# The first loads of a one-core attention and GLU kernel: tile 0 in two column halves, tile 1 from the scalar queue, tiles 2 and 3 ahead of K's weight rows, nine dummy matmuls

## The chip, the core and the metric

The kernel runs on one core of a Trainium2 chip. The core has five engines that run their own instruction lists and meet at semaphores: TensorE (PE, the matrix array; PEld is its weight load), VectorE (DVE), ScalarE (ACT), GpSimd (POOL) and SyncE (SP, which here only issues DMAs). The metric is the device time of one execution in microseconds (us), given as the median of several runs. Times inside an execution are counted from the start of the profile's span.

## The reference

A layer norm without gain or bias feeds two branches, whose outputs are added to the input: attention over a sliding, dilated window (32 heads of 20, 8 positions 2 apart), and a bilinear gated unit without an activation.

```python
def _A_ref(x, wqkv, wo):                 # B, S, D = 1, 2048, 640
    qkv = (x @ wqkv).reshape(B, S, 3, H, Dh) ...
    q, k, v = qkv[0], qkv[1], qkv[2]
    off = jnp.arange(W) * dil            # W, dil = 8, 2
    idx = pos[:, None] - off[None, :]
    ...
    logits = einsum("bhsd,bhswd->bhsw", q, kg) * Dh ** -0.5
    attn = softmax(where(mask, logits, -1e9), axis=-1)
    o = einsum("bhsw,bhswd->bhsd", attn, vg)
    return o.reshape(B, S, D) @ wo

def _B_ref(x, w_gate, w_up, w_down):     # F = 1536
    return ((x @ w_gate) * (x @ w_up)) @ w_down

xn = _layernorm(x)
return x + _A_ref(xn, A_wqkv, A_wo) + _B_ref(xn, B_w_gate, B_w_up, B_w_down)
```

`A_x` is the input of both branches. All arrays are bfloat16.

## The kernel before

The 2048 rows are cut into 16 tiles of 128 rows (`t`), and four blocks of 512 rows (`j`). The 640 columns are five chunks of 128.

**A planner writes the order.** Nothing is issued by hand loops alone. `Sched` keeps, for each engine, a clock of its own (`K.t`), gives each operation an assumed occupancy (`occ`), and each DMA an assumed landing (`land`, where one is given). Threads yield tasks with priorities, and `run` always takes the task that can start first, with the priority deciding between those that are close. The outcome is a fixed list for each engine, with semaphore waits between them; on the chip every engine runs its list in order. So an assumed time costs no instruction, but a different one can change the order of all work behind it. DMAs issued directly, outside a task, stand at the point of the program where they are called.

**The stages.** `front(t)` normalizes a tile: two `bn_stats` of 320 columns each (L574) and an aggregate (L577) on DVE, a square root on ACT (L584), a reciprocal (L591) and the apply on DVE (L603 for tiles 0 and 1, in two pieces of 256 and 384 columns; L606 for tiles 2 to 5) or on ACT (L609, tiles 6 to 15). Tiles 0 to 3 are transposed on PE (L642) and copied from PSUM to `XNT` by ACT or DVE (L653, L655, L662); tiles 4 to 15 are transposed by a DMA on SP's queue (L675). The statistics of tile 1 are planned only after tile 0's apply.

`proj_qk` projects Q and K. For tiles 0 and 1 it uses `spread` (L730), 128 columns at a time, in two parts: chunks 0 and 1, then chunks 2 to 4, for each of the five output groups. Later tiles use L698, as V does. The rows of `wqkv` come in two loads for Q (`wqkv_load(0, ...)`) and two for K (`wqkv_load(1, ...)`): chunks 0 to 2 (480 KB) and chunks 3 and 4 (320 KB). A matmul waits for the load of its own chunk.

Then come the products of Q and K on DVE (L881, and L930 in single precision), their sums on POOL, and the logits on PE, where three blocks of L1013 matmuls reduce over the head dimension; the softmax; the weighted values (L1192 on DVE, added pairwise on POOL at L1197); four groups of L1251 matmuls on PE that sum over the window; the gate and up projections (L1315); and the down and output projections (L1416, L1467), accumulated in one PSUM bank. The gate, up and V projections and parts of the down projection serve as filler between the others.

**The head of the program.** Before the planner runs, the first DMAs are issued in a written order (L1521 to L1529): tile 0 on SP; a small read of `wqkv` (`touch`, 5 KB) on ACT's queue; then, all on SP, Q's first rows, tile 1, Q's last rows, K's first rows, tile 2, K's last rows. `loads` goes on with tile 3. `warm` (L682) puts ten matmuls of constants, 512 columns wide, on PE, into a PSUM bank that nobody reads; three narrower ones stand behind tile 0's transposes.

`x_load(t)` is one DMA of a tile's 128 rows of 640 columns, 160 KB, into a slot of `XST`.

Of the kernel before, what the change touches and what calls it, by code (L numbers as in the profile page):

```python
# [11 lines left out]
NCH = 5  # L12
# [9 lines left out]
TS = 128  # L22
JB = 512
HB = 1024
QB = 256
DHALF = D // 2
# [329 lines left out]
def build_kernel(nc, A_x, A_wqkv, A_wo, B_x, B_w_gate, B_w_up, B_w_down, out):  # L356
    K = Sched(nc)
# [4 lines left out]
    def sb(name, shape, dtype=BF16, at=None):  # L362
        n = mybir.dt.size(dtype)
        for s in shape[1:]:
            n *= s
        n = (n + 63) // 64 * 64
        if at is None:
            at = place[0]
            place[0] += n
        assert at + n <= 229344, (name, at + n)  # L370
        return K.sbuf(name, shape, dtype, at)
# [10 lines left out]
    NXS = 12  # L382
    XST = sb("XST", [128, NXS, D], at=a_ot + NCH * JB * 2)
# [77 lines left out]
    def mark(*k):  # L461
        done.add(k)
# [4 lines left out]
    def have(*k):  # L467
        return lambda: k in done

    def num(n, *k):  # L470
        return lambda: count.get(k, 0) >= n

    xhbm = A_x[0]
    ohbm = out[0]

    def dma(o, i, r=(), w=(), name="", eng="sp", group=None, land=None):
        n = mybir.dt.size(o.dtype)
        for s in o.shape:
            n *= s
        return op(eng, lambda e: e.dma_start(o, i), r=r, w=w, dma=True, name=name, nbytes=n, group=group, land=land)  # L480
# [6 lines left out]
       r=[IDENT[:]], w=[IDENT[:]], name="ident", occ=0.4)  # L487
    op("pool", lambda e: e.memset(SEL[:], 0.0), w=[SEL[:]], name="sel", occ=0.1)
    for q in range(4):
        op("pool", (lambda q: lambda e: e.affine_select(SEL[:], SEL[:], pattern=[[-1, 32]], compare_op=ALU.not_equal, fill=1.0,  # L490
                                                        base=-32 * q, channel_multiplier=1))(q),
           r=[SEL[:]], w=[SEL[:]], name=f"sel{q}", occ=0.2)
# [3 lines left out]
       r=[G[:]], w=[G[:]], name="g1", occ=0.3)  # L496
    op("pool", lambda e: e.affine_select(G[:], G[:], pattern=[[-4, H]], compare_op=ALU.is_ge,
                                         fill=0.0, base=0, channel_multiplier=1),
       r=[G[:]], w=[G[:]], name="g2", occ=0.3)
# [8 lines left out]
    def xslot(t):  # L508
        return t + 4 if t < 8 else t - 8

    def x_load(t, eng="sp", land=None):
        dma(XST[:, xslot(t), :], xhbm[t * TS:(t + 1) * TS, :], w=[XST[:, xslot(t), :]], name=f"xld{t}", eng=eng, land=land)
        mark("x", t)

    wqkv_src = A_wqkv.rearrange("(c p) n -> p c n", p=128)

    def wqkv_load(g, lo=0, hi=NCH, eng="sp", land=None):
        dst = WQKV[:, WPOS[g], lo:hi, :]
        dma(dst, wqkv_src[:, lo:hi, g * D:(g + 1) * D], w=[dst], name=f"ld_wqkv{g}_{lo}", eng=eng, land=land)

    def loads():
        def t(f, *a):
            return Task("sp", lambda: f(*a), prio=0)

        for t_ in range(3, NXS):
            yield t(x_load, t_)
        yield t(wqkv_load, 2)
        for t_ in range(NXS, NT):
            yield have("apply", t_ - NXS)
            yield t(x_load, t_)  # L530

        def w(T, src):
            dma(T[:], src.rearrange("(c p) n -> p c n", p=128), w=[T[:]], name="ld_w")

        def pads():
            z = ZERO[:, 0:PAD].unsqueeze(1).to_broadcast([128, NCH, PAD])
            dma(vscr[:, 0:PAD].rearrange("(c p) s -> p c s", p=128), z, r=[ZERO[:, 0:PAD]], w=[("vscr", "pad")], name="vpad")

        yield have("xnt", NT - 1)
        yield t(w, WG, B_w_gate)  # L540
        yield t(pads)
        yield t(w, WU, B_w_up)

        def copy_x():
            a, b = ohbm[0:3 * JB, :], xhbm[0:3 * JB, :]
            o, i = a.rearrange("(p r) n -> p (r n)", p=128), b.rearrange("(p r) n -> p (r n)", p=128)
            op("sp", lambda e: e.dma_start(o, i), w=[("outx",)], dma=True, name="outx", nbytes=2e6)

        yield num(2, "lg")
        yield t(copy_x)  # L550
# [15 lines left out]
    def front(t):  # L566
        x, st = XST[:, xslot(t), :], STATS[:, t, 0:12]
        xs, mv = XNS[:, t % NXN, :], MV[:, t, 0:2]
        sd, rstd, nmr = SD[:, t, 0:1], SD[:, t, 1:2], SD[:, t, 2:3]
        p = 0.1 * t  # L570

        def stats(i):
            o, a = st[:, 6 * i:6 * i + 6], x[:, i * DHALF:(i + 1) * DHALF]
            op("dve", lambda e: e.bn_stats(o, a), r=[a], w=[("st", t, i)], name=f"bn{t}_{i}", occ=0.49)  # L574
# [4 lines left out]
        ts = next((g for g in GROUPS if t in g), (t,))  # L579
        t0, t1 = ts[0], ts[-1] + 1  # L580

        def sqrt():
            o, i = SD[:, t0:t1, 0:1], MV[:, t0:t1, 1:2]
            op("act", lambda e: e.activation(o, i, ACT.Sqrt, bias=EPSC[:, 0:1]), r=[("mv", k) for k in ts] + [EPSC[:]],  # L584
               w=[("sd", k) for k in ts], name=f"sd{t}", occ=0.25)
            for k in ts:
                mark("sd", k)

# [27 lines left out]
        for i in range(2):  # L616
            if t == 2 and i == 0:
                yield have("apply", 1)
            if t == 2 and i == 1:
                yield have("xnt", t - 1)  # L620
            if t in BN_AFTER and i == 1:
                yield have("rstd", t - 1)
            yield Task("dve", lambda: stats(i), r=[x], prio=p)
        yield Task("dve", aggr, r=[("st", t, 1)], prio=p)
        mark("mv", t)
        if t == ts[-1]:
            yield Task("act", sqrt, r=[("mv", t)], prio=p - 1)
            yield Task("dve", recip, r=[("sd", t)], prio=p)
# [51 lines left out]
    def warm(n, cols=QB):  # L680
        for _ in range(n):
            op("pe", lambda e: e.matmul(PS[:, 7, 0:cols], nc.const_aps.tensor(1.0, (128, 128), BF16), nc.const_aps.tensor(1.0, (128, cols), BF16),  # L682
                                        start=True, stop=True), w=[PS[:, 7, :]], name="warm", occ=0.427 if cols > QB else 0.12)
# [834 lines left out]
    H_PRIO = 9  # L1518
    FIN_PRIO = 8

    x_load(0, land=3.2)  # L1521
    tch = A_wqkv.rearrange("(c k p) n -> k c p n", k=16, c=NCH)[:, :, 0, 0:32]
    stores.append(dma(TCH[0:16], tch, w=[TCH[0:16]], name="touch", eng="act"))
    wqkv_load(0, 0, 3, land=5.3)
    x_load(1, land=5.7)
    wqkv_load(0, 3, NCH, land=7.0)
    wqkv_load(1, 0, 3, land=8.5)
    x_load(2, land=9.0)
    wqkv_load(1, 3, NCH, land=10.0)  # L1529
    K.t["act"] = 2.1  # L1530
    warm(10, JB)

    def misc():
        yield have("xnt", NT - 1)
# [5 lines left out]
        yield Task("act", lambda: op("act", preload, name="exp_preload", occ=1.3), prio=6)  # L1540

    K.spawn(loads())
    for t in range(NT):
        K.spawn(front(t))
# [19 lines left out]
def bass_parallel_sum__sliding_local_dilated__glu_gated_bilinear__prompt_kernel(  # L1564
    nc, A_x, A_wqkv, A_wo, B_x, B_w_gate, B_w_up, B_w_down, out
):
    build_kernel(nc, A_x, A_wqkv, A_wo, B_x, B_w_gate, B_w_up, B_w_down, out)
# [28 lines left out]
```

## Time and profile before

| | us |
|---|---|
| median of 3 runs | 265.16 (265.14 to 265.65) |
| the profiled execution | 265.01 |
| its span | 263.3 |
| granted TensorE clock, share of full speed | 1.00 |

Engines in four stretches of the span, from the table of busy times by stretch (PE's busy time in each):

| stretch, us | PE busy, us | what runs there |
|---|---|---|
| 0.86 to 4.20 | 3.34 | dummies |
| 4.20 to 5.30 | 0.60 | the last dummies, then idle |
| 5.30 to 8.21 | 2.86 | tile 0 and 1: transposes and first projections |
| 8.21 to 35.07 | 26.76 | projections, while the front goes on |
| 35.07 to 261.04 | 224.49 | everything else |

The costliest groups of the page, columns: line, engine, operation, output and input tile, shapes, count; busy us and mean ns of one; idle us just before them and what ended it:

```profile
L1197 POOL TENSOR_TENSOR SV<-PV 128x1024 bf16<-128x1024 f32 x40 | 94.2, 2522 | 15.7 <-DVE HT L1362 3.6
L698 PE MATMUL PS<-XNT,WQKV 128*128 128x512 bf16 (+2 forms) x384 | 60.0, 316 | 0.5 <-issue 0.3
L1315 PE MATMUL PS<-XNT,WU 128*128 128x512 bf16 x239 | 59.4, 379 | 0.2 <-issue 0.2
L574 DVE BATCH_NORM_STATS2 STATS<-XST 128x6 f32<-128x320 bf16 x32 | 14.0, 470 | 2.4 <-DMA XST<-in_A_x_dram 2.4
```

A group's busy time says how much of the span one line takes; its idle time says how long its engine stood still just before it. Idle time matters only on the engine that is the bound. A matmul's length of 379 ns includes the time until its result is written; the next one starts after about 216.

DMA issues, columns: destination and source, queue, count, size of one, median us from issue to landing:

```profile
XST<-in_A_x_dram SPq DMA_DIRECT2D x16, 160.0 KB, 5.3
ATX<-LOG SPq DMA_DIRECT2D x32, 32.0 KB, 2.0
TCH<-in_A_wqkv_dram ACTq DMA_DIRECT2D x1, 5.0 KB, 2.5
```

The first issues, taken one by one: tile 0, issued at 0.82, lands after 2.4; Q's first rows, issued at 1.27, after 3.7; tile 1 (1.73) after 3.7; Q's last rows (2.25) after 4.0; K's first rows (2.73) after 5.4; tile 2 (3.24) after 5.3; K's last rows (3.78) after 5.7; tile 3 (4.26) after 5.7.

### The profile page before, as it was taken

Reading aid. Unit: us, or ns where it says so; the run is one execution under the profiler, and the core shown is the slowest. Engines: PE = TensorE matmul, PEld = TensorE weight load, DVE = VectorE, ACT = ScalarE, POOL = GpSimd, SP = SyncE. Lnnn points to the kernel's source line nnn. Section 1 sums busy time; section 2 is a strip of 40 time slices with the busy share of each in tenths; the row PEclk is TensorE's granted clock in tenths of the full one; section 3 lists DMA queues with packets and bytes.
Section 4 is the critical chain, followed back from the end, with each engine's and each line's share of the span. In section 5 each row is a group of like instructions: output and inputs, shape, how many; then the busy total and the mean of one; then the engine's idle time right before and its main releaser. Section 6 shows DMA issues by size and latency. Waiting matters only on the chain.

```text
span 263.3 us, 4080 instructions
## 1 busy us (share of the span) xinstructions
PE 258.1 (98%) x1566; PEld 135.9 (52%) x1587; DVE 218.9 (83%) x259; ACT 112.8 (43%) x198; POOL 160.6 (61%) x97
## 2 busy tenths in 40 slices
PE   7999999999999999999999999999999999999996
PEld 3996965444444444444444444444444444445675
DVE  4687899999998798778779999999999989994041
ACT  3559987556612221224258656521350144211300
POOL 3000000000599998899973576799989999999100
PEclk9999999999999999999999999999999999999999
DMA  6964699970479996470249424847779676721621
GB/s 212 373 218 81 121 104 366 416 281 12 122 133 186 217 229 129 88 142 1 62 129 309 88 47 109 169 113 171 177 174 208 149 162 137 110 55 37 94 62 50
DMA packets 47843, 39.78 MB, mean 151 GB/s; under 512 B 23856, under 2 KB 45488, under 8 KB 47792
## 3 DMA queue, kind: packets, MB, share of 16 engines
q1 hardware_dynamic: 44848, 33.29, 49.5%
q0 software_dynamic: 2736, 6.16, 13.6%
q8 instruction: 12, 0.20, 0.3%
q10 hardware_dynamic: 240, 0.07, 0.1%
q14 instruction: 7, 0.06, 0.1%
HBM read 25.07 MB, written 7.23 MB: 123 GB/s over the span
## 4 chain that ended last, share of the span: by engine, by line
PE 91%; ACT 6%; issue 1%; DMA 1%; DVE 1%
PE PS L1315 39%; PE PS L1416 21%; PE PS L698 17%; PE PS L1467 7%; ACT XNS L609 3%; PE PS L730 2%; PE PS L1013 2%; PE PS L1251 2%; DMA XST<-in_A_x_dram 1%; ACT QT L703 1%; PE PS L642 1%; ACT VST L703 1%; ACT KT L703 1%; ACT SD L584 0%; DVE STATS L574 0%
## 5 line engine op out<-in xcount | busy, mean ns | idle before, releaser
L1197 POOL TENSOR_TENSOR SV<-PV 128x1024 bf16<-128x1024 f32 x40 | 94.2, 2522 | 15.7 <-DVE HT L1362 3.6
L1192 DVE TENSOR_TENSOR PV<-VX,PS 128x1024 f32<-128x1024 bf16 (+1 forms) x54 | 90.9, 1729 | 2.3 <-POOL SV L1197 2.3
L698 PE MATMUL PS<-XNT,WQKV 128*128 128x512 bf16 (+2 forms) x384 | 60.0, 316 | 0.5 <-issue 0.3
L1315 PE MATMUL PS<-XNT,WU 128*128 128x512 bf16 x239 | 59.4, 379 | 0.2 <-issue 0.2
L1315 PE MATMUL PS<-XNT,WG 128*128 128x512 bf16 x231 | 57.7, 379 | 0.6 <-ACT LOG L1024 0.2
L698 PEld LDWEIGHTS PS<-XNT,WQKV 128*128 128x128 bf16 x390 | 37.8, 112 | 21.9 <-ACT LOG L1024 0.8
L930 DVE TENSOR_TENSOR PRF<-PS,KT 128x1024 f32<-128x1024 f32 x32 | 37.9, 1217 | 0.3 <-PE PS L698 0.3
L1315 PEld LDWEIGHTS PS<-XNT,WU 128*128 128x128 bf16 x240 | 23.4, 98 | 28.5 <-ACT OT L1260 0.4
L1315 PEld LDWEIGHTS PS<-XNT,WG 128*128 128x128 bf16 x240 | 23.4, 98 | 28.5 <-issue 0.4
L956 POOL TENSOR_TENSOR PRF<-PRF,PRF 128x1024 f32<-128x1024 f32 x8 | 22.0, 2751 | 20.6 <-DVE LOG L1073 20.6
L703 ACT ACTIVATE HT<-PS 128x512 bf16<-128x512 f32 x24 | 14.3, 597 | 34.5 <-PE PS L1315 34.5
L881 DVE TENSOR_TENSOR PRD<-QT,KT 128x2048 bf16<-128x2048 bf16 x24 | 27.3, 1223 | 0.0
L1416 PE MATMUL PS<-HT,WD 128*128 128x512 bf16 x117 | 27.2, 380 | 0.1
L1032 POOL MEMSET LOG<- 32x6 bf16 (+6 forms) x7 | 0.4, 95 | 43.7 <-ACT LOG L1024 43.7
L703 ACT ACTIVATE UX<-PS 128x512 bf16<-128x512 f32 x15 | 9.0, 597 | 40.6 <-PE PS L1416 40.6
L989 POOL TENSOR_TENSOR PRD<-PRF,PRF 128x1024 bf16<-128x1024 f32 x8 | 21.4, 2759 | 0.1
L967 POOL TENSOR_TENSOR PRF<-PRF,PRD 128x1024 f32<-128x1024 f32 x8 | 19.5, 2544 | 0.0
L1416 PEld LDWEIGHTS PS<-HT,WD 128*128 128x128 bf16 x120 | 11.7, 98 | 14.3 <-ACT OT L1260 0.4
L1416 PE MATMUL PS<-OT,WO 128*128 128x512 bf16 x75 | 18.6, 379 | 0.1
L1480 DVE TENSOR_TENSOR FB<-PS,XR 128x320 bf16<-128x320 f32 (+2 forms) x9 | 4.1, 455 | 17.4 <-PE PS L1467 16.9
L1324 DVE TENSOR_TENSOR HT<-HT,PS 128x512 bf16<-128x512 bf16 x18 | 12.3, 684 | 7.0 <-PE PS L1315 7.0
L574 DVE BATCH_NORM_STATS2 STATS<-XST 128x6 f32<-128x320 bf16 x32 | 14.0, 470 | 2.4 <-DMA XST<-in_A_x_dram 2.4
(76 smaller groups left out, 246.4 us busy)
## 6 DMA issues: line engine op xcount, KB each, us to landing
VX<-v_scratch SPq DMA_DIRECT2D x80, 130.0 KB, 3.0
PRF<-PRF POOLq DMA_DIRECT2D x8, 512.0 KB, 5.1
XST<-in_A_x_dram SPq DMA_DIRECT2D x16, 160.0 KB, 5.3
v_scratch<-VST SPq DMA_DIRECT2D x4, 640.0 KB, 6.3
WG<-in_B_w_gate_dram SPq DMA_DIRECT2D x1, 1920.0 KB, 9.8
WU<-in_B_w_up_dram SPq DMA_DIRECT2D x1, 1920.0 KB, 14.0
out_dram<-in_A_x_dram SPq DMA_DIRECT2D x1, 1920.0 KB, 20.0
WD<-in_B_w_down_dram SPq DMA_DIRECT2D x1, 1920.0 KB, 8.1
```

Of the source, the lines that this page charges most:

```text
L698: op("pe", (lambda o, l, x, c, first: lambda e: e.matmul(o, l, x, start=first, stop=(c == NCH - 1)))(o, l, x, c, first), r=[l, x], w=[o], ...
L703: X = op("act", (lambda o, i: lambda e: e.activation(o, i, ACT.Copy))(o, i), r=[i], w=[o], name=name, occ=0.12 + n * 0.9e-3)
L881: op("dve", lambda e: e.tensor_tensor(s[:], qb, kv, ALU.mult), r=[q, rk], w=[s[:]], name=f"prod{j}_{r}_{c}", occ=1.15, lock=True)
L930: X = op("dve", lambda e: e.tensor_tensor(o[:], qb, kv, ALU.mult), r=[q, rk, ("qev", j, c)], w=[o[:]], name=f"prow{j}_{r}_{c}_{q0}", occ=1.17)
L956: yield Task("pool", lambda: op("pool", lambda e: e.tensor_tensor(x, x, y, ALU.add), r=[x, y] + tokens(), w=[x], name=name, occ=2.36, lock ...
L967: yield Task("pool", lambda: op("pool", lambda e: e.tensor_tensor(x, x, z, ALU.add), r=[x, z] + tokens(), w=[x], name=name + "c", occ=2.36 ...
L989: yield Task("pool", lambda: op("pool", lambda e: e.tensor_tensor(o, a, y, ALU.add), r=[a, y] + tokens(), w=[o], name=f"qend{j}_{r}_{q0}", ...
L1192: last[0] = op("dve", lambda e: e.tensor_tensor(p, vw, a, ALU.mult), r=[vv] + rk, w=[p], name=f"pv{u}_{x}_{r0}", occ=0.09 + 1.1 * nr)
L1197: X = op("pool", lambda e: e.tensor_tensor(o, p[:, :, 0, :], p[:, :, 1, :], ALU.add), r=[p[:]] + tokens(), w=[o], name=f"pva{u}_{x}", occ= ...
L1315: op("pe", (lambda l, x, c: lambda e: e.matmul(PS[:, b, :], l, x, start=(c == 0), stop=(c == NCH - 1)))(l, x, c), r=[l, x], w=[PS[:, b, :] ...
L1416: op("pe", (lambda l, x, i: lambda e: e.matmul(PS[:, b, :], l, x, start=(i == 0), stop=(i == n - 1)))(l, x, i), r=[l, x], w=[PS[:, b, :]], ...
L1467: op("pe", (lambda l, x, i: lambda e: e.matmul(dst, l, x, start=(i == 0), stop=(i == n - 1)))(l, x, i), r=[l, x], w=[PS[:, b, :]], name=f" ...
```

## The change

Tile 0 is loaded by two DMAs of 320 columns each, both on SP; its two statistics are planned, and wait, for their own half. Tile 1 is issued on ACT's queue, behind the touch. Q's first and last rows follow each other on SP; tile 2 stands ahead of K's first rows, tile 3 ahead of K's last rows, and `loads` starts with tile 4. The assumed landings are set anew, the planned occupancy of the square root is 0.36 in place of 0.25, the planner's clock of ACT starts at 2.5 in place of 2.1, and there are nine wide dummies in place of ten.

```diff
+    def x_half(i, land):
+        c = slice(i * DHALF, (i + 1) * DHALF)
+        dma(XST[:, xslot(0), c], xhbm[0:TS, c], w=[XST[:, xslot(0), c]], name=f"xld0_{i}", land=land)
+        if i:
+            mark("x", 0)
...
-        for t_ in range(3, NXS):
+        for t_ in range(4, NXS):
             yield t(x_load, t_)
...
-               w=[("sd", k) for k in ts], name=f"sd{t}", occ=0.25)
+               w=[("sd", k) for k in ts], name=f"sd{t}", occ=0.36)
...
-            yield Task("dve", lambda: stats(i), r=[x], prio=p)
+            yield Task("dve", lambda: stats(i), r=[x[:, i * DHALF:(i + 1) * DHALF]] if t == 0 else [x], prio=p)
...
-    x_load(0, land=3.2)
+    x_half(0, land=2.84)
     tch = A_wqkv.rearrange("(c k p) n -> k c p n", k=16, c=NCH)[:, :, 0, 0:32]
     stores.append(dma(TCH[0:16], tch, w=[TCH[0:16]], name="touch", eng="act"))
-    wqkv_load(0, 0, 3, land=5.3)
-    x_load(1, land=5.7)
-    wqkv_load(0, 3, NCH, land=7.0)
-    wqkv_load(1, 0, 3, land=8.5)
-    x_load(2, land=9.0)
-    wqkv_load(1, 3, NCH, land=10.0)
-    K.t["act"] = 2.1
-    warm(10, JB)
+    x_half(1, land=3.3)
+    x_load(1, land=4.0, eng="act")
+    wqkv_load(0, 0, 3, land=5.45)
+    wqkv_load(0, 3, NCH, land=6.5)
+    x_load(2, land=6.9)
+    wqkv_load(1, 0, 3, land=8.6)
+    x_load(3, land=9.0)
+    wqkv_load(1, 3, NCH, land=9.9)
+    K.t["act"] = 2.5
+    warm(9, JB)
```

## The prediction

> **What bounds the kernel now.** The profiled execution took 265.01 us, of which the instructions span 263.3; the other 1.71 us lie around them and are kept. The median of the three runs is 265.16, so 0.15 is added to a sum made against the profile. I read the busy times and the chain's shares first:
>
> ```profile
> PE 258.1 (98%) x1566; PEld 135.9 (52%) x1587; DVE 218.9 (83%) x259; ACT 112.8 (43%) x198; POOL 160.6 (61%) x97
> PE 91%; ACT 6%; issue 1%; DMA 1%; DVE 1%
> ```
>
> TensorE is the bound, but matmul ends are modelled, so I asked for all waits of PE:
>
> ```profile
> PE PS L682 <- PEq L1581: 0.9, 1, 0.9
> PE PS L642 <- DVE XNS L603: 0.5, 1, 0.5
> PE PS L698 <- issue: 0.3, 2, 0.2
> PE PS L1315 <- issue: 0.2, 1, 0.2
> PE PS L1315 <- ACT LOG L1024: 0.2, 1, 0.2
> ```
>
> The reader should see a list that ends after five rows: once real matmuls run, PE idles 0.7 us in 250. A transfer, a statistic or an evacuation that comes sooner after that can save next to nothing. What can be saved lies ahead of it, in the chain of waits in order of time:
>
> ```profile
> 0.82 2.36 DMA XST<-in_A_x_dram
> 3.18 0.02 issue
> 3.20 0.90 DVE STATS L574 x2
> 4.10 0.02 issue
> 4.12 0.22 DVE MV L577
> ...
> 4.90 0.36 DVE XNS L603
> 5.25 0.05 issue
> 5.30 0.29 PE PS L642 x2
> ...
> 8.21 3.54 PE PS L730 x60
> ...
> 261.04 0.29 DVE FB L1480
> ```
>
> Tile 0 lands at 3.18, its statistics end at 4.10, its first transpose starts at 5.30, tile 1's come 2.2 later, and from 8.21 PE never waits long. Whatever pulls 4.10 forward pulls the whole run forward, microsecond for microsecond, if nothing new stops PE.
>
> **Tile 0 in halves (gain).** Two stats of 0.45 each can start when the first 80 KB are there. No row shows such a load, so I bound it. The small SBUF copies ATX<-LOG (32 KB) land after a median 2.0 us, tile 0 itself (160 KB) after 2.36. On the line between them 80 KB take 2.0 + 48/128 x 0.36 = 2.14. Issues on SP stand 0.45 apart (0.82, 1.27, 1.73), so the halves land at 0.82 + 2.14 = 2.96 and 1.27 + 2.14 = 3.41. The stats then end at the later of 2.96 + 0.02 + 0.90 = 3.88 and 3.41 + 0.02 + 0.45 = 3.88, against 4.10: **0.22 us gained**. With 2.0 for both it would be 0.36 (the first half decides: 2.82 + 0.92 = 3.74). The dear end is the 5 KB touch, issued at 0.83, which took 2.5: the second half would land at 3.77, the stats end at 4.24, a loss of 0.14. The rate of the first 8 us, in steps of 0.2, warns of that end too:
>
> ```profile
> GB/s 0 0 0 0 0 0 0 0 0 83 45 245 373 284 96 83 256 358 397 403 378 397 397 371 397 390 371 390 256 173 243 301 314 378 390 397 378 352 365 378
> ```
>
> After tile 0's burst (2.2 to 2.8) come two steps at 96 and 83: a second transfer does not start at full rate. If it costs the second half those 0.4 us behind a burst that ends at 2.6, it still lands near 3.5. I keep 0.22.
>
> **Tile 1 on the ACT queue (nothing).** ACT's queue is:
>
> ```profile
> 0.83 0.40 ACTq L480 DMA_DIRECT2D TCH<-in_A_wqkv_dram  x1
> 1.26 1.28 ACT L584 ACT_TABLE_LOAD   x1 [1.26 <-PEq L1581]
> 4.37 0.30 ACT L584 ACTIVATE SD<-MV,EPSC 128x1 f32<-128x1 f32 x1 [1.82 <-DVE MV L577]
> ```
>
> The issue (0.40 to 0.49) goes between the first two; the table load ends near 3.05 instead of 2.54, and the square root behind it is wanted at 4.37 - 0.22 = 4.15. The cover is 1.1 us; without it each late microsecond would be on the chain. The load lands between 1.27 + 2.4 and 1.27 + 3.7 = 4.97 (the time it took on SP), and its stats start at 5.45 - 0.22 = 5.23, since they stand behind tile 0's apply on DVE.
>
> **Q rows behind that (nothing, cover 0.2 to 0.4).** Q's first three chunks, issued at 1.27, landed 3.7 later, at 4.97. Now the issue is third (1.73) and tile 1's 160 KB run beside it. At 390 KB a microsecond that is 0.41, so 5.4; if the later issue counts in full as well, 5.85. PE wants them at 6.10 - 0.22 = 5.88. The last two chunks keep the fourth place (2.25, 4.0 to landing: 6.25) with the same bytes ahead; PE reaches them 15 matmuls of 0.056 after 5.88, at 6.72. Beyond these covers a late landing costs its full excess.
>
> **Tiles 2 and 3 ahead of K's rows (nothing).** Tile 2 changes places with K's first rows: 480 KB fewer ahead of it, at 390 KB a microsecond 1.2 us sooner than 3.24 + 5.3 = 8.5, and DVE's one further wait for a tile (2.4 us in two, 1.97 of it for tile 0: 0.45) goes. PE does not collect it: tile 2's apply ended at 10.75 and its transposes ran at 11.59. K's first rows take tile 2's old landing, 8.5; wanted at 7.99 + 25 x 0.056 = 9.39. K's last take tile 3's old one, 4.26 + 5.7 = 9.96. In the new order 45 projection matmuls, tile 2's transposes (5) and 5 more stand before the first that needs them: 7.99 + 55 x 0.056 = 11.1. SP's queue has as many issues ahead of tile 4 as before.
>
> **Nine dummies (nothing, or the clock).** The tenth dummy of 512 columns starts at 4.42, PE idles from 4.80 to 5.30, and the transposes will start at 5.08; nine leave PE free 0.22 sooner and idle for the same 0.5. Idle time hides the removal; what it could cost is the clock:
>
> ```profile
> 3.37 0.15 PEld L682 LDWEIGHTS PS<-const-bfloat16-1.0 128*128 128x128 bf16 x1 [0.28 <-issue]
> 3.80 0.15 PEld L682 LDWEIGHTS PS<-const-bfloat16-1.0 128*128 128x128 bf16 x1 [0.28 <-issue]
> 4.20 0.10 PEld L682 LDWEIGHTS PS<-const-bfloat16-1.0 128*128 128x128 bf16 x1 [0.26 <-issue]
> ```
>
> Dummies are 0.43 apart until 3.80; at 4.20 the weight load shortens from 0.15 to 0.10, and the next dummy follows after 0.22. PE went to full rate about 3.35 after it began. Eight dummies had started before that, so nine suffice if the next run switches at the same place.
>
> The Trainium skill ("TensorE: Matmul & The Clock Gate", Part 1: The HAM clock gate) speaks against this part. It says that PE runs at half rate until a busy window of 3.4 us has passed, and that the window is free-running, so the switch moves from run to run. The one profile agrees with the length; no trace here shows it moving. By the row the sum is unchanged; by the rule one run in some eight (0.43 of 3.4) would lose up to 1.7 us, an estimate from that page.
>
> **The re-planned order (nothing, with small covers).** The new occupancy of the square root (0.36 for 0.25) issues no instruction, but with the new landings the planner orders all later work anew. PE's own work stays the same but for one dummy. The first logits block moves up by 10 matmuls of 0.216, or 2.16 us, the second by 1.08; of the four sums groups (L1251) the second moves back by 1.08, the third up by 2.16, the fourth by 12 x 0.136 = 1.63. Each needs its producers that much sooner:
>
> ```profile
> 31.66 13.71 DVE L881 TENSOR_TENSOR PRD<-QT,KT 128x2048 bf16<-128x2048 bf16 x12
> 213.98 4.67 POOL L1197 TENSOR_TENSOR SV<-PV 128x1024 bf16<-128x1024 f32 x2 [0.16 <-DVE PV L1192]
> 238.77 4.66 POOL L1197 TENSOR_TENSOR SV<-PV 128x1024 bf16<-128x1024 f32 x2 [0.16 <-DVE PV L1192]
> ```
>
> The tenth product ended at 31.66 + 10 x 1.14 = 43.1; the last of the ten steps of the first block, at 46.4 before, now comes at 44.0. Pool's thirtieth add ended at 218.65; the third sums stood at 221.54, now at 221.54 - 2.16 - 0.22 = 219.16. The fortieth ended at 243.43; the fourth sums come at 246.08 - 1.85 = 244.23. So even if DVE and Pool gain nothing, covers of 0.9, 0.5 and 0.8 us remain, and I put down nothing. Below zero there is no room: PE had no stall there to lose.
>
> **Sum.** 265.01 - 0.22 = 264.79 against the profile; against the median 265.16 - 0.22 = 264.94, say **264.9**. Its own range is 264.8 (0.36 gained) to 265.3 (0.14 lost).
>
> **Rivals.** (1) *The second half is no sooner than the whole was.* For: the touch's 2.5 and the two slow steps. Against: half the bytes, and tile 0's own 2.36. From a landing at 3.63 the gain is nil: 265.1 to 265.3. Chance 0.17. (2) *Pool's third sums become PE's wait: slower.* The place is L1251 at 219.2, the cover 0.5. One add more ahead of it on Pool (2.36 us, from the same rows) makes PE wait 1.86 with every down-projection behind it: 265.16 - 0.22 + 1.86 = 266.8; half an add late gives 265.6. It decides once the thirtieth add ends after 219.2. For: DVE's products that feed Pool are reordered among the softmax and the gate multiplies. Against: the same count of adds stands ahead, and tiles 2 onward are ready sooner. Chance 0.14. (3) *The clock stays at half rate into the projections.* The 25 matmuls from 6.26 (1.40 us) would take 2.8, so 266.3 if it lasts that long. For: one dummy less. Against: 3.80 to 4.20 above. Chance 0.08. (4) *PE gains more than I see*, if tile 1's chain, whose apply makes PE wait between 7.5 and 8.21, also closes up by its pauses there (0.16 + 0.20 beyond five transposes of 0.056): 264.94 - 0.36 = 264.6. Against: each step of tile 1 stands on DVE behind tile 0's, and none is removed. Chance 0.16.
>
> **Numbers.** The forecast has 0.45. A change of 0.2% is 0.53 us, about what a measurement of this kernel can tell from none: faster means below 264.63, slower above 265.69. The forecast and rival 1 lie within, but for scatter such as the runs' own 265.14 to 265.65, which I give a fifth of the forecast on the fast side, as it is the side it leans to: faster 0.16 + 0.08 = 0.24; slower 0.14 + 0.08 less a small share that stays inside, 0.20; same 0.56. The range leaves out the far end of rivals 2 and 3 and the fastest scatter: 264.4 to 265.7.
>
> **What would show it.** Right: two stats that start near 3.0 and end near 3.9, a first transpose near 5.1, the 45 projections from 8.0, and a list of PE's waits no longer than before. Wrong: stats that wait for DMA twice and end after 4.1; PE waiting for Q's rows near 5.9; weight loads of 0.15 us after the first transpose; or PE L1251 or L1013 in the list of waits, released by Pool or DVE.

## The result, and the profile after

The changed kernel takes 266.19 us (median of 12 executions, 265.87 to 267.95), the kernel before beside it on the same chip 265.22 (12, 265.14 to 265.65). The ratio of the means is 1.005, interval [1.0029, 1.0071]: slower by half a per cent (by 0.97 us in the medians), and above the range of the forecast. The twelve times fall into two groups: eight lie between 265.87 and 266.67, four between 267.66 and 267.95.

The profiled execution is one of the four, at 267.95, so its account is 267.95 - 265.01 = 2.94 us. The page's busy times and the chain's shares by engine:

```profile
PE 261.2 (98%) x1586; PEld 137.4 (52%) x1586; DVE 219.0 (82%) x259; ACT 112.7 (42%) x198; POOL 160.7 (60%) x97
PE 93%; DVE 3%; DMA 1%; POOL 1%; issue 1%; ACT 0%; SPq 0%
```

PE is busy 3.1 us longer, though it has one dummy less to do. A part of that may be records that are missing before (1566 matmuls for 1587 weight loads); the rest has to be slower matmuls somewhere. All of PE's waits (engine, line, what ended the wait, total us, times, longest us):

```profile
PE PS L648 <- DVE XNS L609: 1.0, 1, 1.0
PE PS L688 <- PEq L1589: 0.9, 1, 0.9
PE PS L1321 <- DVE XNT L1330: 0.7, 1, 0.7
PE PS L736 <- DVE XNT L659: 0.2, 1, 0.2
```

(A helper of six lines was added ahead of these lines, so each one's number is 6 higher than before: L648 are the transposes, L688 the dummies, L736 the first projections, L1321 the gate and up projections.) Two things are new. The wait ahead of the first transpose is 1.0 instead of 0.5, and there is a wait of 0.7 at a gate projection, which ended when the gate multiply L1330 on DVE had run. The chain of waits, in order of time (start us, us, what):

```profile
1.27 2.86 DMA XST<-in_A_x_dram
...
4.16 0.51 DVE STATS L580
...
5.86 0.79 PE PS L648 x5
6.65 0.64 PE PS L688 x3
7.29 2.62 PE PS L736 x25
...
10.41 2.71 PE PS L736 x45
...
172.63 0.69 DVE XNT L1330
...
173.37 1.25 PE PS L1321 x5
...
263.98 0.29 DVE FB L1486
```

Three losses add up. (a) The second half of tile 0, issued at 1.27, took 2.86 us and landed at 4.14, later than the whole tile did (3.18): the first transpose starts at 5.86 instead of 5.30, 0.56 lost. (b) 25 projection matmuls take 2.62 us, some 0.105 each, where they took 0.056 apiece before, and the five transposes and three narrow dummies ahead of them are slow too (0.79 and 0.64, before 0.63 and 0.33); the 45 projections (60 in a row before) start at 10.41 instead of 8.21, 2.20 later, of which 2.20 - 0.56 = 1.64 is this. (c) PE stands still for 0.7 at 172.7. The sum is 2.90 of 2.94.

The table by stretches shows (b) as a rate. After the stretch come its length, then PE's busy time and count, the weight loads', DVE's, ACT's and POOL's, PEclk, DMA share and GB/s. The changed kernel:

```profile
7.00:9.90 2.90, 2.90 (x30) 2.83 (x29) 0.93 (x4) 0.46 (x2) 0.00 (x0) 1.00 1.07 381
```

The same stretch of a version with the same loads and the old order (E2 below):

```profile
7.00:9.90 2.90, 2.86 (x47) 2.48 (x45) 2.12 (x8) 1.53 (x4) 0.00 (x0) 1.00 1.07 376
```

PE was busy throughout in both, but finished 30 matmuls instead of 47. The column of the granted clock says 1.00 both times, so the slow rate has to be read from the pace.

For (c), the timeline of the kernel before at that place (start us, us, engine, line, operation, tiles, count):

```profile
169.23 1.26 PE L1251 MATMUL PS<-SV,SEL 128*32 128x512 bf16 x20
...
170.43 2.76 PE L1416 MATMUL PS<-HT,WD 128*128 128x512 bf16 x12
170.80 0.68 DVE L1324 TENSOR_TENSOR XNT<-XNT,PS 128x512 bf16<-128x512 bf16 x1
171.40 4.48 DVE L1192 TENSOR_TENSOR PV<-VX,PS 128x2048 f32<-128x2048 bf16 x2
```

and of the changed one:

```profile
171.45 1.26 PE L1257 MATMUL PS<-SV,SEL 128*32 128x512 bf16 x20
171.50 1.21 DVE L1198 TENSOR_TENSOR PV<-VX,PS 128x1024 f32<-128x1024 bf16 x1
...
172.63 0.68 DVE L1330 TENSOR_TENSOR XNT<-XNT,PS 128x512 bf16<-128x512 bf16 x1
...
173.37 1.25 PE L1321 MATMUL PS<-XNT,WG 128*128 128x512 bf16 x5 [0.65 <-DVE XNT L1330]
```

Before, twelve down-projection matmuls stand behind the first sums group (L1251). They add into a bank that is theirs, and the gate multiply beside them has time. Now the planner puts a gate projection there. It writes a PSUM bank that the gate multiply still has to read, and on DVE a weighted-value product of 1.21 us stands ahead of that multiply. So the gate projection waits for a bank, not for data: the multiply also writes into `XNT`, but into columns of another block than the one that the projection reads.

### The profile page after: what moved, and what is told of

The parts are those of the page before. It is cut to its first block, busy times and chain, and to the rows that moved or that the text cites. A ratio compares the mean times of both kernels' runs of the same rounds, so it can differ in the third digit from the quotient of the medians.

```text
span 266.2 us, 4099 instructions
## 1 busy us (share of the span) xinstructions
PE 261.2 (98%) x1586; PEld 137.4 (52%) x1586; DVE 219.0 (82%) x259; ACT 112.7 (42%) x198; POOL 160.7 (60%) x97
## 4 chain that ended last, share of the span: by engine, by line
PE 93%; DVE 3%; DMA 1%; POOL 1%; issue 1%; ACT 0%; SPq 0%
PE PS L1321 36%; PE PS L704 22%; PE PS L1422 21%; PE PS L1473 7%; PE PS L736 3%; PE PS L1019 2%; PE PS L1257 1%; DVE PV L1198 1%; DMA XST<-in_A_x_dram 1%; POOL SV L1203 1%; PE PS L648 1%; DVE XNT L1330 1%; DVE XNT L1368 0%; PE PS L688 0%; ACT ZERO L709 0%
## 5 line engine op out<-in xcount | busy, mean ns | idle before, releaser
L704 PE MATMUL PS<-XNT,WQKV 128*128 128x512 bf16 (+2 forms) x390 | 60.7, 316 | 0.0
L1321 PE MATMUL PS<-XNT,WG 128*128 128x512 bf16 x240 | 59.7, 379 | 0.7 <-DVE XNT L1330 0.7
L1321 PE MATMUL PS<-XNT,WU 128*128 128x512 bf16 x240 | 59.6, 379 | 0.0
L1321 PEld LDWEIGHTS PS<-XNT,WG 128*128 128x128 bf16 x240 | 23.2, 98 | 29.6 <-DVE XNT L1330 1.6
L1321 PEld LDWEIGHTS PS<-XNT,WU 128*128 128x128 bf16 x240 | 23.5, 98 | 28.3
L962 POOL TENSOR_TENSOR PRF<-PRF,PRF 128x1024 f32<-128x1024 f32 x8 | 21.3, 2663 | 21.8 <-DVE LOG L1079 21.8
L1330 DVE TENSOR_TENSOR HT<-HT,PS 128x512 bf16<-128x512 bf16 x18 | 12.3, 685 | 7.2 <-PE PS L1321 7.1
```

The lines of the kernel that those rows point to most:

```text
L704: op("pe", (lambda o, l, x, c, first: lambda e: e.matmul(o, l, x, start=first, stop=(c == NCH - 1)))(o, l, x, c, first), r=[l, x], w=[o], ...
L962: yield Task("pool", lambda: op("pool", lambda e: e.tensor_tensor(x, x, y, ALU.add), r=[x, y] + tokens(), w=[x], name=name, occ=2.36, lock ...
L1321: op("pe", (lambda l, x, c: lambda e: e.matmul(PS[:, b, :], l, x, start=(c == 0), stop=(c == NCH - 1)))(l, x, c), r=[l, x], w=[PS[:, b, :] ...
```

## The experiments

In each kernel below, all engine lists are those of its base except for the edit shown; where a load was moved but not the order, the assumed landings and the planner's clocks were set so that the later order came out unchanged. `x_half` is the helper of the change, and is not shown again. Each ratio is against the kernel before, run on the same chip beside it.

**E1: the changed kernel again.** No edit.

> The changed kernel, unedited. Its first profile lost 2.9 us of PE's end in three places: 0.56 up to the first transpose (second half of tile 0 landed at 4.14), 1.64 between the first transpose and the 45 projections (tile 0's 25 matmuls took 2.8 us in place of 1.6, about half rate), 0.72 in one PE wait at 172.6. Theory 1 (late half, then half rate, then a planned-order wait): times again fall in two groups, near 265.9 and 267.7, and a profile of the lower group has 25 projections in 1.4 to 1.6 us with the wait at 172 still there. Theory 2 (one fixed cause, the order): all runs alike.

Measured: 266.16 (six executions, 265.83 to 266.97), ratio 1.0038 [1.0025, 1.0051]. None of the six is near 267.7, so a profile of the lower group is at hand (266.31). The second half lands at 3.60, the first transpose starts at 5.33, the 45 projections at 8.77, and PE waits 0.8 at L1321. The account: 8.77 - 8.21 = 0.56 in the head and 0.8 at the gate projection, 1.36 against 266.31 - 265.01 = 1.30. The late wait is in both groups. A part of the slow pace is as well: the first transpose is only 0.03 late, and the other 0.53 of the head is lost behind it, as the chain shows:

```profile
5.33 0.79 PE PS L648 x5
6.12 0.64 PE PS L688 x3
6.76 1.51 PE PS L736 x25
...
8.77 2.71 PE PS L736 x45
```

Transposes and narrow dummies are as slow as in the upper group; the projections are at the full pace from the fourth on, near 6.8. Only in the upper group do all 25 take double the time.

**E2: all loads of the change and nine dummies, in the order of before.** Against the kernel before:

```diff
-        for t_ in range(3, NXS):
+        for t_ in range(4, NXS):
...
-    x_load(0, land=3.2)
+    x_half(0, land=3.2)
...
+    x_half(1, land=3.2)
+    x_load(1, land=5.7, eng="act")
     wqkv_load(0, 0, 3, land=5.3)
-    x_load(1, land=5.7)
     wqkv_load(0, 3, NCH, land=7.0)
-    wqkv_load(1, 0, 3, land=8.5)
     x_load(2, land=9.0)
+    wqkv_load(1, 0, 3, land=8.5)
+    x_load(3, land=10.585)
     wqkv_load(1, 3, NCH, land=10.0)
...
-    warm(10, JB)
+    warm(9, JB)
+    K.t["pe"] += 0.427
```

> All of the change's DMAs, halves and nine dummies, with the planner's assumed landings and occupancies set so that every engine's list of work is that of the kernel before. Theory 1: no PE wait near 172, so 0.7 below the changed kernel, 265.2 to 267.2 in two groups by the clock. Theory 2 (only the order costs): 265.2 or a little less, one group.

**E3: the order of the change, with the loads of before and ten dummies.** Against the changed kernel:

```diff
+        yield t(x_load, 3, "sp", 9.0)
...
-    x_half(0, land=2.84)
+    x_load(0, land=2.84)
...
-    x_half(1, land=3.3)
-    x_load(1, land=4.0, eng="act")
     wqkv_load(0, 0, 3, land=5.45)
+    x_load(1, land=4.0)
     wqkv_load(0, 3, NCH, land=6.5)
-    x_load(2, land=6.9)
     wqkv_load(1, 0, 3, land=8.6)
-    x_load(3, land=9.0)
+    x_load(2, land=6.9)
...
-    warm(9, JB)
+    warm(10, JB)
+    K.t["pe"] -= 0.427
```

> The change's order of work on every engine with the loads and ten dummies of the kernel before. Theory 1: the head is that of before (first transpose 5.30, 45 projections from 8.2), and the wait near 172 remains: 265.2 + 0.7 = 265.9, no group near 267.7. Theory 2: the whole loss, 266.2. Rival (the wait at 172 comes from the late head, not from the order): 265.2.

E3 took 265.97 (five, 265.89 to 266.26), ratio 1.003 [1.0019, 1.0042]: 0.83 us slower, though its head is that of before (first transpose 5.25, 45 projections 8.25). Its profile has the wait behind the gate multiply, until 171.8 (one more line was added there, hence L1322):

```profile
PE PS L1322 <- DVE XNT L1331: 0.9, 1, 0.9
```

E2 took 265.55 (twelve), ratio 1.0037 [1.0016, 1.0058], with seven executions from 265.12 to 265.57 and five from 266.87 to 267.83; its profile (265.32) has no late wait. Run a second time, to count the groups better:

> All the change's DMAs and nine dummies in the old order of work once more, on the chip of the next two, to set them against it. Five of its twelve executions lay at 266.9 to 267.8, the others at 265.1 to 265.6. If the half rate is a property of this head, again a third to a half of them above 266.5.

it gave 265.44 (eleven), ratio 1.0019 [1.0, 1.0037], three of them from 266.82 to 267.42. So the order costs some 0.8 in every execution, and the loads with nine dummies cost little in most and 1.5 or more in 8 of 23. The two are separate.

**E9: one planned number.** The kernel before, with the square root's planned occupancy alone; no instruction is changed.

```diff
-               w=[("sd", k) for k in ts], name=f"sd{t}", occ=0.25)
+               w=[("sd", k) for k in ts], name=f"sd{t}", occ=0.36)
```

> The kernel before with the planned occupancy of the square root at 0.36 in place of 0.25: loads, dummies and instructions as before, the order of the later work changed by the planner. As in the changed kernel, a gate projection now stands directly behind the first sums group. Theory (that placement makes PE wait for a bank that a gate multiply on DVE still holds): a PE wait of 0.7 to 0.9 near 171, 265.9 to 266.0. Rival (the wait needs the rest of the new order): 265.15 or less.

Measured: 266.1 (ten, 265.87 to 266.3) against 265.41, ratio 1.0029 [1.002, 1.0038]. Its list of PE's waits has one row that the list of before lacks (its line numbers are those of before):

```profile
...
PE PS L1315 <- DVE XNT L1324: 0.6, 1, 0.6
```

Its timeline at that place:

```profile
169.57 1.26 PE L1251 MATMUL PS<-SV,SEL 128*32 128x512 bf16 x20
169.61 1.22 DVE L1192 TENSOR_TENSOR PV<-VX,PS 128x1024 f32<-128x1024 bf16 x1
170.74 0.68 DVE L1324 TENSOR_TENSOR XNT<-XNT,PS 128x512 bf16<-128x512 bf16 x1
...
171.47 1.25 PE L1315 MATMUL PS<-XNT,WG 128*128 128x512 bf16 x5 [0.64 <-DVE XNT L1324]
```

The sums group, the weighted-value product, the gate multiply and the waiting gate projection stand in the same order as after the change, and cost 0.64 of wait out of the 0.69 by which the kernel got slower. No run puts that one projection back and leaves the rest of the new order, so the evidence is that its wait is nearly the whole loss. An assumed tenth of a microsecond at the head decides which projection stands at 170 us. The number does not explain the change's order alone: in the planned order of the changed kernel, which was read but not run, the gate projection stands there with 0.25 as well.

**E6: nine dummies alone**, on the kernel before, and **E7: the changed kernel with thirteen.**

```diff
-    warm(10, JB)
+    warm(9, JB)
+    K.t["pe"] += 0.427
```

> The kernel before with nine dummies, nothing else (lists as before). If the half rate comes from the missing dummy itself, some runs lie 1 to 2 us above the rest, and the median above 265.3; if it takes the late transposes of the split tile as well (PE idle for over 1 us), 265.15 in one group, as before.

```diff
-    warm(9, JB)
+    warm(13, JB)
+    K.t["pe"] -= 4 * 0.427
```

> The changed kernel with 13 dummies in place of nine, all lists otherwise the same. If the half rate comes from PE standing still from 4.6 to 5.9 with the transposes late, 13 dummies (to 5.3 at full rate) leave the idle time that the kernel before had, and the group near 267.7 goes: 265.9. If it comes from where the clock's window falls and not from the idle time, the two groups stay. If dummies delay the transposes, above 265.9 by what they overhang 5.1 to 5.9.

E6 took 265.42 (eleven, 265.27 to 265.64) against 265.41, ratio 1.0004 [0.9995, 1.0013]. E7 took 266.47 (five, 265.94 to 266.74), ratio 1.0047 [1.0034, 1.006]: no time near 267.7, and the late wait stays. **E10** puts thirteen dummies into E2:

> The same with 13 dummies in place of nine, lists otherwise the same. Theory (half rate comes from too little work on PE before the late transposes): no execution above 266.5, and a median near 265.4, which is the lower group's. Rival (where the clock switches is chance, dummies or not): a third of the executions above 266.5.

It took 265.46 (eleven, 265.18 to 266.09), ratio 1.001 [1.0001, 1.0018], none in the upper group. Together 0 of 16 with thirteen dummies (E7, E10) stand against 8 of 23 with nine and the change's loads (E2 twice), 0 of 11 with nine dummies and the loads of before (E6), and 0 of 11 with ten dummies, halves and tile 1 on ACT's queue (E14 below). So the upper group came only with nine dummies and the change's loads together. Thirteen are no cure. The chain of E10's slowest execution, the profiled one, at its head:

```profile
0.86 5.71 PE PS L688 x13
6.56 0.33 PE PS L648 x5
6.90 0.33 PE PS L688 x3
7.23 1.57 PE PS L736 x25
```

Here PE did not pause, and yet the pace doubled only near 6.5; so thirteen dummies at half rate last until then and hold the transposes up. A late switch thus came with thirteen too. It cost 9.29 - 8.21 = 1.08 at the 60 projections, all of 266.09 - 265.01, and so stays below the upper group.

**E4: halves alone.** The kernel before, with tile 0 in two DMAs on SP.

```diff
-    x_load(0, land=3.2)
+    x_half(0, land=3.2)
...
+    x_half(1, land=3.2)
+    K.t["sp"] -= 0.48
```

> The kernel before with tile 0 in two halves on SP, nothing else: tile 1 stays on SP, ten dummies, every engine's list of work as before. So far the second half landed at 3.6 to 4.1, against 3.13 to 3.18 for the whole tile. Theory 1a (it is slowed by tile 1's load, which runs beside it from ACT's queue): it lands near 3.3, and PE's end comes 0.1 to 0.2 sooner: 265.0. Theory 1b (a second transfer of a queue starts slowly by itself, whatever runs beside it): it lands after 3.6, 265.5 or more.

**E5: tile 1 on ACT's queue alone.**

```diff
+    x_load(1, land=5.7, eng="act")
...
-    x_load(1, land=5.7)
+    K.t["sp"] += 0.48
```

> The kernel before with tile 1's load moved to ACT's queue behind the touch, nothing else (lists as before). Theory 1a: tile 1 runs beside whatever SP issued at the same time; tile 0 is ahead of it and lands near 3.2, but Q's first rows land later than 4.98, by up to 0.5; PE wants them at 6.10, so 265.1 to 265.2. Rival (tile 1 delays tile 0 as it did the second half): tile 0 after 3.4, 265.4 or more.

E5 took 265.2 (eleven, 265.13 to 265.56) against 265.41, ratio 0.9993 [0.9984, 1.0001]: nothing, as forecast. E4 took 266.6 (five, 266.04 to 266.92) against 265.41, ratio 1.0042 [1.003, 1.0055], 1.2 us slower, although tile 0 did what was forecast: halves at 2.83 and 3.16, first transpose at 5.07. PE's waits of E4 have a row of weights:

```profile
PE PS L736 <- DMA WQKV<-in_A_wqkv_dram: 0.5, 2, 0.3
PE PS L648 <- DVE XNS L609: 0.5, 1, 0.5
```

The second row is the wait until 8.43 ahead of tile 1's transposes: tile 1 lands at 6.31 instead of 5.42. The chain of waits runs through K's last rows:

```profile
4.24 7.84 DMA WQKV<-in_A_wqkv_dram
...
12.13 1.31 PE PS L736 x20
```

The rate of its first 8 us, in steps of 0.2:

```profile
GB/s 0 0 0 0 0 0 0 0 0 106 212 165 219 141 67 45 26 70 102 237 301 384 390 403 371 378 384 378 403 390 339 288 218 256 262 346 307 333 314 320
```

From 2.8 to 3.8 the rate is 26 to 102 GB/s; in the profile of before, that hole was two steps long (96 and 83). Only 51 packets of the DMA queues started in that microsecond, 189 in the profile of before; 14 of the 51 took 260 to 1102 ns, most of the others 55. Q's first rows land at 5.86 instead of 4.97, K's last at 12.08 instead of about 9.5, and K's last rows now set the end of the head. The 0.23 gained at the first transpose is paid back several times over. It could have been 0.36, as the statistics ended at 3.74 instead of 4.10 and the apply's first piece at 4.89; but in this profile all ten dummies ran at the slow pace and held PE until 5.07.

**E14: halves and tile 1 on ACT's queue**, E4 with E5's edit:

> The kernel before with tile 0 in two halves on SP and tile 1 on ACT's queue; ten dummies, K's rows and tiles 2 and 3 where they were, old order of work. Against the halves alone it differs by tile 1's queue only. If tile 1 beside it is what delays the second half, it lands at 3.6 to 4.1 (3.16 alone), stats end at 4.1 to 4.7, and no half-rate group (ten dummies) or a smaller one: 265.2 to 265.9. If not, it lands near 3.2 and the time is 265.0.

265.5 (eleven, 265.10 to 266.31), ratio 1.0013 [1.0004, 1.0022]. The long lull and K's late landing (9.38 now) are gone, but so is the gain, as its chain begins to show:

```profile
1.28 2.36 DMA XST<-in_A_x_dram
...
3.67 0.51 DVE STATS L580
...
5.37 0.28 PE PS L648 x2
```

The second half, issued at 1.28, took 2.36 and landed at 3.65; in E4, issued at 1.27, it took 1.9 and landed at 3.16. In seven profiles with tile 1's load beside it on ACT's queue the second half landed at 3.60, 3.63, 3.65, 3.78, 3.90, 4.14 and 4.18. **E11** keeps the change's loads and makes tile 0 whole again, with ten dummies and the order of before. Against E2:

```diff
-    x_half(0, land=3.2)
+    x_load(0, land=3.2)
...
-    x_half(1, land=3.2)
+    K.t["sp"] += 0.48
...
-    warm(9, JB)
-    K.t["pe"] += 0.427
+    warm(10, JB)
```

> The change's loads without the halves and with ten dummies: whole tile 0, tile 1 on ACT's queue, tiles 2 and 3 ahead of K's rows, old order of work. Theory (halves plus nine dummies carry all the loss of the loads): tile 0 near 3.3, first transpose near 5.4, 265.1 to 265.4, none above 266. Rival (tile 1's queue or the new sequence costs too): above 265.5.

265.18 (eleven, 265.10 to 265.31), ratio 0.9995 [0.9986, 1.0003]: the other loads' new order and queue cost nothing, and gain nothing.

**E8 and E13: halves on two queues.** To keep the second half from standing second on SP, it was issued first on ACT's queue (E8, tile 1 on SP); in E13 tile 1 follows it on ACT's queue.

```diff
-    x_load(0, land=3.2)
+    x_half(0, land=3.2)
+    K.t["act"] = 0.8
+    dma(XST[:, xslot(0), DHALF:D], ..., eng="act", land=3.2)
+    x_load(1, land=5.7, eng="act")
```

(the last line in E13 alone, in place of tile 1's load on SP; `...` stands for the rest of the call)

> The kernel before with tile 0 in halves on two queues, the second from ACT ahead of the touch, so that both are issued at 0.82 and Q's first rows keep their issue at 1.27; ten dummies, old order of work. Halves alone on SP landed at 2.83 and 3.16 and brought the first transpose to 5.07, but Q's first rows came at 5.86 for 4.98 and K's at 10.73 for 8.15. Theory (the weights were late because a third issue stood ahead of them): both halves near 2.9, transposes near 5.0, Q's rows near 5.1, 264.9 to 265.0, a version ahead of both kernels. Rival (small rows ahead of them slow the weights' start, on whatever queue): Q's rows after 5.5, 265.3 or more.

> Halves on two queues as before, with tile 1 third, on ACT's queue behind the second half and ahead of the touch. With tile 1 on SP the halves landed at 2.91 and 3.07, but its stats waited for tile 1's landing at 5.57 and Q's last rows. If tile 1's landing is what ate the 0.3, it now lands by 4.8, tile 1's transposes start near 7.3 and PE ends 0.2 to 0.3 sooner than before: 264.9 to 265.0. If transfers side by side share the rate so that Q's rows come after 5.8 instead, 265.2 or more: then the head cannot be shortened by reordering these loads.

E8: 265.27 (twelve, 265.01 to 266.01), ratio 0.9999 [0.999, 1.0007]; E13: 265.39 (eleven, 264.93 to 265.49), ratio 1.0003 [0.9994, 1.0012]. The halves land at 2.91 and 3.07 in E8, 3.05 and 3.21 in E13, and the first transposes start at 5.03 and 5.17. Yet the 60 projections behind tile 1's transposes start at 8.36 and 8.40. E13's chain says why:

```profile
1.26 4.35 DMA XST<-in_A_x_dram
...
5.64 0.90 DVE STATS L580 x2
...
7.73 0.28 PE PS L648 x2
...
8.40 3.54 PE PS L736 x60
```

Tile 1, issued third of all big loads at 1.26, takes 4.35 us and lands at 5.61. For its statistics DVE was free from 5.40. The lateness has moved from tile 0 to tile 1. No version was found that beats the kernel before.

## Why the prediction was wrong

The sign was wrong, and the time lies outside the range. Step by step:

- **"Tile 0 in halves (gain)" failed.** Alone on SP the halves did better than it said: the statistics ended at 3.74 in E4, forecast 3.88, which is the good end of its bound (0.36). That the first transpose at 5.07 fits the forecast 5.08 is luck, since there dummies and not data held PE. The step failed in two ways that the sum treated as free. The landing of the second half, put at 3.41, was worked out without tile 1's 160 KB beside it, which stood in the next step of the same text; with it 3.60 to 4.18 were measured (without it 3.16, in the one profile of E4), past the dear end of 3.77 in four of seven profiles. And without tile 1 moved away, one more small load in front costs the weights 0.9 to 2.6 us and tile 1 0.9. The two slow steps in the rate row were read as a delay for one transfer; in E4 the second half landed at 3.16 all the same, and a longer hole held up the loads behind it.
- **"The re-planned order (nothing, with small covers)" failed, and is the larger part.** It cost 0.83 in E3 and 0.69 in E9. The step checked whether every logits and sums group would find its data in time, and that held: no wait at L1257 or L1019 appears. It did not ask which PSUM bank each moved projection would write, and who still had to read it. Rival 2 looked at the right place, the sums groups, but named Pool (and took 2.36 for an add where its rows give 4.67 / 2 = 2.33, which changes nothing); the releaser is the gate multiply on DVE, and the waiting line is the projection behind the group.
- **"Nine dummies (nothing, or the clock)": rival 3, held at 0.08, came true.** One execution of the upper group was profiled and shows it; by their times it is 4 of 18 executions of the changed kernel (4 of 12, then 0 of 6) and 8 of 23 of its loads in the old order. The price of 1.4 was near what the profiled execution lost, 1.64; it left out the transposes and narrow dummies ahead of the 25 matmuls. A shorter spell of half rate, 0.53 in E1's profile, hides in the lower group. The step let nine dummies "leave PE free 0.22 sooner and idle for the same 0.5"; as the second half came late, PE idled 1.0 us (4.86 to 5.86). That nine suffice if the switch comes at the same place was read from a single profile. The Trainium skill ("TensorE: Matmul & The Clock Gate", Part 1: The HAM clock gate) calls the window free-running, and spoke against this step; the profiles agree that the switch moves from execution to execution (the last section has the times), and the counts of upper executions are higher than the one in eight that the prediction worked out with the page's figure.
- **Rival 1, "the second half is no sooner than the whole was", was also true**: 3.60 and 4.14 in the two profiles of the changed kernel, against 3.18. The first is as it was priced (no gain: the first transpose at 5.33 for 5.30), the second worse (5.86).
- **Right:** tile 1 on ACT's queue (E5), tiles 2 and 3 ahead of K's rows, and Q's rows cost nothing by themselves (E11). Nothing behind 8.21 gains.

The sum with the terms as measured: order +0.8, head between +0.2 and +0.4 (E2's medians against those beside them), together 1.0 to 1.2. The changed kernel lost 266.19 - 265.22 = 0.97, and 266.16 - 265.14 = 1.02 in E1. So the order and the late second half set the median; rival 3 accounts for the four upper executions. Of the signs of being wrong that the prediction named, two showed in the profile of the result: statistics that waited twice and ended at 4.65, and weight loads of 0.15 us after the first transpose, until 9.5. The late wait stands at a line that it did not name.

Open: what puts off the switch to full rate. An idle stretch of 1.0 us ahead of the first transpose went with the latest switch, but idle time does not decide it alone: E2 and E5 idled 0.82 and ran at the full pace from the first transpose on, E6 idled 0.59 and E1 0.48 and switched near 6.6 and 6.8, E10 did not idle and switched near 6.5. The upper executions of E2 were not profiled; that they too are late switches is inferred from their times. Also open is what makes the hole in the load rate of E4.

## What to carry to other kernels

When a planner sets the order, an assumed duration is part of the kernel: after any change of it, list for each moved instruction not only its producers but the reader that has to leave its buffer. A load that is made to land sooner must be priced together with every load that the same change puts beside it, and the next load in the chain must be sooner too, or the lateness only changes its name. Warm-up work that just suffices in one profile has no margin: count how many executions fall short, and read the pace of the first matmuls, not the granted clock.

## What the runs showed of the hardware

- **The switch of PE to full rate moves.** PE starts at 0.86 in all these kernels. The pace doubled near 4.0 to 4.2 (before, E5, E9, E14), 4.4 (E11), 4.7 (E7), 5.3 (E4), 6.5 to 6.8 (E10, E6, E1) and only near 9.7 in the profiled execution of the changed kernel, while the granted clock read 1.00. The timeline of that last one, in its head:

```profile
0.86 4.00 PE L688 MATMUL PS<-const-bfloat16-1.0 128*128 128x512 bf16 x9 [0.86 <-PEq L1589]
...
7.09 2.82 PE L736 MATMUL PS<-XNT,WQKV 128*128 128x128 bf16 x25
```

Nine dummies in 4.00 us are 0.44 each, about double the 0.22 of a dummy at full rate, and the 25 projections still have the slow pace.

- **A load on one queue delays a load on another.** The 80 KB second half took 1.9 us with only SP's loads behind it (E4) and 2.3 to 2.9 with 160 KB more on ACT's queue; the 160 KB of tile 1 issued at 1.26 in E13 took 4.35, where tile 0's 160 KB, first on SP, took 2.31 to 2.50 in the four profiles with the loads of before (before, E3, E6, E9). How far one profile differs from the next can be seen there: the same load scattered by 0.2.
